# The lead-in of a recurrent-memory layer: fewer and larger DMA stores on one queue, and fewer warming products in the layer before it

## The chip, the cores and the metric

The kernel runs on one core of one Trainium2 chip. The metric is the device time of one execution in microseconds (us). The core has five engines that each run their own list of instructions: TensorE (PE) with its weight loads (PEld), VectorE (DVE), ScalarE (ACT), GpSimd (POOL) and SyncE (SP). DMAs are issued by an engine as one of its instructions (here almost all by SP, and some by ACT) and are carried by 16 shared DMA engines. An instruction that waits for a semaphore holds up all that stands behind it on its engine, a DMA issue among them.

## The reference

Four residual layers in a row, A, B, A, B, on x of 2048 rows by 640 columns, each behind a layer norm without weights:

```python
x = x + _A_ref(_layernorm(x), A_wq, A_wk, A_wv, A_wo, A_beta)
x = x + _B_ref(_layernorm(x), B_mem0, B_Wq, B_Wk, B_Wv, B_Wo, B_seg_len)
x = x + _A_ref(_layernorm(x), ...)
x = x + _B_ref(_layernorm(x), ...)
```

A is attention with a compressive memory: 32 heads of 20, four segments of 512 rows; in each, causal-masked softmax attention, and beside it a read of a memory matrix that the earlier segments' keys and values were added to; the two are mixed by a gate, sigmoid of beta. B is a recurrent-memory transformer, 32 heads of 128, in 64 segments of 32 rows:

```python
mem = mem0                                    # 8 tokens
for s in range(64):
    h = concatenate([mem, x[32*s : 32*s+32]])  # 40 tokens
    q, k, v = h @ Wq, h @ Wk, h @ Wv
    p = softmax(where(mask, q @ k.T * scale, -1e9))
    o = (p @ v) @ Wo
    mem = o[:8]                               # feeds the next segment
    outs.append(o[8:])
```

The 64 steps of B depend on one another through `mem`, so they run one after the other.

## The kernel before

**A.** The work runs over 32 groups of four heads (`NGR`), in a loop over `g` from 0 to `NGR + 1`; each group's scores (S, tiles `a_S`) are made in one turn, and its transposed scores, exponentials and products with V (T, tiles `a_T`, `a_PT`, `a_PV`) two turns later. So in the last two turns, `g >= NGR`, only T rounds are left: the drain. `unread(k)` sends k products of 128x256 to PE into a tile `a_W` that nothing reads. It is called at the start of the layer, ahead of each of the four blocks of transposes of the normed input (`seg_tr`), in the drain ahead of each round (nine times in a layer), and in a few other places. The order of ACT, DVE and POOL in A comes from due times (`KeyOrder`, `A_LAGS`): an instruction's key is its turn plus a lag by kind.

**B.** One step: projections of K and Q in two halves each (`b_Ka`, `b_Qa`, `b_Kb`, `b_Qb`), transposes of them (`b_TPak` and so on), scores `b_SP`, V in two halves (`b_Va`, `b_Vb`), the transposed probabilities (`b_PTP`), the product with V (`b_OTP`), the output product with Wo (`b_OPS`), and the new memory's transposes (`b_MT`) into `b_HX`, from which the next step's projections read. In B the order of PE, ACT, DVE and POOL is the order in which the instructions are written (`_OrdNC`); SP's is the scheduler's.

A step carries 40 tokens but the step's products are made for 32 of them, the 8 of memory and the first 24. The last eight of each segment, the tails, don't depend on memory; their Q, K and V are made ahead of time, for eight segments at once, a batch T for segments 8T to 8T+7. `tail_unit` and `tail_evac` make a batch's Q and K in eight pieces, k = 0 to 7 (tile `b_tail` in PSUM, `b_tu` in SBUF), and store each into DRAM at `QKd`. `vtail_unit` and `vtail_evac` do the same for V (`b_vtail`, then `b_vt` or `b_vts`), stored to `VTd`. Each step reads its own tails back: `tails_load` (tile `b_tl`), `tails_copy` (POOL, into `b_QZ` and `b_KT`), and `vtails_in` (four DMAs into rows of `b_Vth`).

**The lead-in of B.** Ahead of step 0 a stretch of code is run once in each B layer: it loads and norms the first four groups of 128 rows (`ln_load`, `ln_norm`; `ln_spread` transposes a normed group into `b_HX` and `b_TX`, tile `b_lntps`), makes the Q and K tails of batch 0 in eight pieces, makes K and Q of step 0's input rows (`b_Kp`, `b_Qp`), loads Wo in eight pieces of 640 KB (`load_B_wo`, `b_wo`), loads the first tails, makes the V tails of batch 0 in eight pieces and V of step 0's input (`b_V`), reads V tails back, and makes the first piece of batch 1. All of these evictions alternate between ACT and DVE. The stores of the pieces are issued by ACT for half of them and by SP for the others:

```python
tail_evac(0, k, "act" if k % 2 == 0 else "dve", ..., (nc.sync if k % 2 else nc.scalar).dma_start)
...
vtail_evac(0, k, vtail_unit(0, k), "dve" if k % 2 == 0 else "act", vt_homes[k], (nc.scalar if k % 2 else nc.sync).dma_start)
```

Each of the eight V pieces is a [128, 256] tile and goes out in two stores of 64 partitions, sixteen in all. `OTdef` are two tiles of [128, 32, 32] that later steps use for deferred output products; during the lead-in they are free.

Of the kernel before, what the change touches and what calls it, by code (L numbers as in the profile page):

```python
# [19 lines left out]
BF16 = mybir.dt.bfloat16  # L20
# [224 lines left out]
def layer_A(nc, tc, C, W, x_src, x_dst, src_is_bf16, nseg=4, out_bf16=False, xb_dst=None, load_w=None, side_loads=None):  # L245
    SC = 1.0 / math.sqrt(20.0)
    nc_raw = nc
    nc = _OrdNC(tc, nc_raw, engines=("tensor",))
# [4 lines left out]
    with ExitStack() as ctx:  # L253
# [15 lines left out]
        wk = pool("a_wk", 2)  # L269
# [34 lines left out]
        def unread(k):  # L304
            W_ = pg.tile([128, 256], F32, name="a_W", tag="pg")
            for _ in range(k):
                nc.tensor.matmul(W_[:], lhsT=C.identb[:], rhs=C.negu[:].rearrange("p a k -> p (a k)"), start=True, stop=True, skip_group_check=True)
# [297 lines left out]
        for tt in range(4):  # L605
            K.base = 0.1 * tt - 100.0
            seg_norm(0, tt)
            K.base = None
            unread((14 if src_is_bf16 else 6, 4, 4, 4)[tt])
            seg_tr(0, tt)  # L610
        K.base = -90.0
        lw.send(K) if src_is_bf16 else None
# [83 lines left out]
        for g in range(NGR + 2):  # L696
            n, G = divmod(g, 8)
            for half in range(2):
                p, tp = 2 * g + half, 2 * g + half - 3
                for ph in range(2):  # L700
                    K.base = 4 * g + 2 * half + ph
                    todo = []
                    for what in VISITS[ph]:
                        kind, r = what[0], int(what[1])
                        if kind == "X":
                            X = s_mask(p, r) if g < NGR else t_tile()
                            if g < NGR:
                                todo.append(("S", p, r, X, 0))
                            if 0 <= tp - 1 < 2 * NGR:
                                todo.append(("T", tp - 1, r, X, 256))  # L710
                        elif kind == "S" and g < NGR:
                            todo.append((kind, p, r, s_mask(p, r), 0))
                        elif kind == "T" and 0 <= tp < 2 * NGR:
                            todo.append((kind, tp, r, t_tile(), 0))
                    for step in range(2):
                        for kind, p_, r, X, o0 in todo:
                            if step == 0 and g >= NGR:
                                unread(4)
                            f = (s_mm, s_max)[step] if kind == "S" else (t_round, t_exp)[step]
                            f(p_, r, X, *((o0,) if o0 else ()))  # L720
                    if g < NGR and half == 1 and ph == 1:
                        negmax_rows(g)
                    if g == NGR + 1 and half == 1 and ph == 0:
                        last_turns(0, 4)
                        for tt in range(4):
                            last_oT(tt, 0, 4, K("last").vector if tt < 2 else nc.scalar)
                    filler(g, 2 * half + ph)
                    if side_loads is not None and g < NGR:
                        if g + half + ph == 0:
                            build_gates(nc, st, W, side_loads[1])  # L730
                        side_loads[0](4 * g + 2 * half + ph, GS[g]["kT"])
# [45 lines left out]
def layer_B(nc, tc, C, W, x_src, xb_src, x_dst, mem0, B_Wv, B_Wo, nsteps=64, out_bf16=False, tag=""):  # L777
    SCB = 1.0 / math.sqrt(128.0)
    nc_raw = nc
    nc = _OrdNC(tc, nc_raw, engines=ORDER_ENGINES)  # L780
# [3 lines left out]
    VTd = tc.dram_tile([nsteps, 8, 4096], BF16, name=f"b_VTd{tag}")  # L784
    with ExitStack() as ctx:
# [8 lines left out]
        kqp = pool("b_kqp", 4)  # L794
        W.wo = pool("b_wo", 1).tile([128, 32, D], BF16, name="b_wo")
        st = pool("b_state", 1)
        w2 = pool("b_w2", 2)
        wk = pool("b_wk", 1)
# [30 lines left out]
        HX, TX, QT, KT, VH = {}, {}, {}, {}, {}  # L829
# [83 lines left out]
                nc.sync.dma_start(VH[s - 1][32 * j:32 * j + 8, :, :],  # L913
                                  VTd[s].rearrange("t (b n e) -> t n b e", b=2, e=512)[:, j, :, :])

        tail_ps, vts = {}, {}

        def tail_unit(T, k, i0, i1, shared=False):
            proj, hg = divmod(k, 4)
# [13 lines left out]
        def tail_evac(T, k, eng, home=None, dma=nc.sync.dma_start):  # L933
            proj, hg = divmod(k, 4)
            pool_, tg = home or (wk, "tu")
            tu = pool_.tile([128, 8, 8, 8], BF16, name="b_tu", tag=tg)
            evac(eng, tu[:].rearrange("p s h t -> p h s t"), tail_ps[0][:].rearrange("p h (s t) -> p h s t", t=8),
                 None if proj else SCB)
            o = 256 * proj + 64 * hg
            dma(QKd[8 * T:8 * T + 8, :, o:o + 64].rearrange("s p f -> p s f"), tu[:].rearrange("p s h t -> p s (h t)"))  # L940

        def vtail_unit(T, k, c0=0, c1=NCH, ps=None):
            b4, ch = divmod(k, 2)
            if ps is None:
                ps = ps_tile([128, 256], F32, "b_vtail")
            for c in range(c0, c1):
                for q in range(4):
                    n = 2 * b4 + q // 2
                    nc.tensor.matmul(ps[32 * q:32 * q + 32, :], lhsT=TX[T][:, c, 4 * (q % 2):4 * (q % 2) + 4, :].rearrange("p s t -> p (s t)"),
                                     rhs=W.wv[:, c, 512 * n + 256 * ch:512 * n + 256 * ch + 256],  # L950
                                     start=(c == 0), stop=(c == NCH - 1), tile_position=(0, 32 * q), skip_group_check=True)
            return ps

        def vtail_evac(T, k, ps, eng, home=None, dma=nc.sync.dma_start):
            b4, ch = divmod(k, 2)
            if isinstance(home, int):
                if home == 0:
                    vts[0] = wk.tile([128, 5, 256], BF16, name="b_vts", tag="OTsb")
                vt = vts[0][:, home, :]
            else:  # L960
                pool_, tg = home or (wk, "vt")
                vt = pool_.tile([128, 256], BF16, name="b_vt", tag=tg)[:]
            evac(eng, vt, ps[:])
            for jj in range(2):
                o = 512 * (2 * b4 + jj) + 256 * ch
                dma(VTd[8 * T:8 * T + 8, :, o:o + 256].rearrange("s t f -> (s t) f"), vt[64 * jj:64 * jj + 64])
# [29 lines left out]
                nc.sync.dma_start(HX[0][:, c, 1, 0:8], mem0[:, 128 * c:128 * c + 128].rearrange("t p -> p t"))  # L996
        for k in range(8):
            tail_unit(0, k, 0, 8, shared=True)
            tail_evac(0, k, "act" if k % 2 == 0 else "dve", (((kqp, "kq"),) * 4 + ((w2, "QT"), (w2, "KT"), (wk, "tu"), (w2, "Vth")))[k],
                      (nc.sync if k % 2 else nc.scalar).dma_start)  # L1000
            if k in (0, 2) and n0 > 2:
                ln_norm(2 + k // 2)
            if k in (3, 5) and ln_ready:
                ln_spread(ln_ready.pop(0))
        cols = cols_of(0)
        jobs = [(nm, b) for b in range(2) for nm in ("K", "Q")]
# [13 lines left out]
        XO, XOd = init_state()  # L1020
        tails_copy(0, tails_load(0))
        Vth = VH[-1] = w2.tile([128, 2, 512], BF16, name="b_Vth", tag="Vth")
        vt_homes = [0, 1, 2, 3, 4] + [(wk, x) for x in ("PTa", "PTb", "E0")]
        for k in range(8):
            vtail_evac(0, k, vtail_unit(0, k), "dve" if k % 2 == 0 else "act", vt_homes[k],
                       (nc.scalar if k % 2 else nc.sync).dma_start)
        for b in range(2):
            ps = thin_mm(cols, W.wv, b, "b_V")
            evac("act" if b == 0 else "dve", Vth[:, b, :], ps[:])
# [372 lines left out]
```

## Time and profile before

| what | value |
|---|---|
| three runs | 2700.09, 2691.12, 2696.44 us |
| median | 2696.44 us |
| profiled execution, its own time | 2692.14 us |
| its span | 2690.4 us |
| mean granted TensorE clock | 0.997 |

By the trace, the first A layer fills about the first 342 us, the first B runs to about 1341, the second A to about 1683, and the second B to the end. A step of B is about 15 us. The stretches that the change touches are the first 20 us and the last 12 us of each A layer, and the lead-in of each B layer, which are the stretches 342 to 400 and 1683 to 1740. A window row of the profile gives the busy time of each engine, the clock that was granted to TensorE as a share of full speed, and how busy the DMA engines were; a chain row gives one piece of work and its duration, on the path that was followed back from the end of the window; a row with `[5.82 <-issue]` says how long the engine was idle ahead of it and what ended that.

### The profile page before, as it was taken

The numbers are of one execution on the slowest core, as the hardware profiler recorded it, in microseconds if no ns is written. First come the engines' busy times: TensorE is split into PE (matmuls) and PEld (weight loads), VectorE is DVE, ScalarE is ACT, GpSimd is POOL, SyncE is SP. The second block draws the span as 40 slices with busy tenths as digits, with TensorE's granted clock in tenths as the row PEclk, the third lists the DMA queues.
The fourth block names the chain that finished last, engine by engine and source line by source line (L and its number), as shares of the span: only waits on it lengthen the run. The fifth ranks groups of instructions, "written<-read, shape, count | busy, mean of one in ns | idle before, by whom it ended". The sixth has DMA issues, their size and how long they took to land.

```text
span 2690.4 us, 147288 instructions
## 1 busy us (share of the span) xinstructions
PE 2576.7 (96%) x65632; PEld 1699.2 (63%) x65632; DVE 1698.4 (63%) x4562; ACT 1583.1 (59%) x3718; POOL 710.0 (26%) x1631
## 2 busy tenths in 40 slices
PE   7999989999999999999989999899999999999998
PEld 5556566666666666666655566666666666666665
DVE  8999845555555555555589998455555555555554
ACT  6988835454555555554479898355555555555543
POOL 5777611111111111111156776111111111111110
PEclk9999999999999999999999999999999999999999
DMA  4122451222222222121120113511212121211110
GB/s 155 45 79 80 139 166 41 44 44 43 44 45 43 45 43 44 41 41 31 54 89 22 61 51 138 164 40 40 43 39 44 41 43 41 42 40 41 38 26 19
DMA packets 326620, 156.37 MB, mean 58 GB/s; under 512 B 246240, under 2 KB 310880, under 8 KB 324192
## 3 DMA queue, kind: packets, MB, share of 16 engines
q1 hardware_dynamic: 316384, 145.38, 21.3%
q8 instruction: 513, 8.40, 1.4%
q10 hardware_dynamic: 9600, 1.57, 0.4%
q14 instruction: 123, 1.01, 0.1%
HBM read 95.15 MB, written 51.71 MB: 55 GB/s over the span
## 4 chain that ended last, share of the span: by engine, by line
PE 79%; DVE 11%; ACT 5%; DMA 2%; issue 2%; SPq 1%; POOL 0%; ACTq 0%; DVEq 0%; POOLq 0%
PE b_OPS L109 11%; PE b_tail L109 5%; DVE a_nm L138 5%; PE b_Qa L109 5%; PE b_Ka L109 5%; PE b_Kb L109 5%; PE b_Qb L109 5%; PE b_Va L109 5%; PE b_Vb L109 5%; PE b_SP L109 4%; PE b_OTP L109 4%; PE b_OPSd L109 3%; PE b_PTP L109 3%; PE b_vtail L109 3%; ACT a_PT L138 3%; PE a_S L109 2%
## 5 line engine op out<-in xcount | busy, mean ns | idle before, releaser
L109 PEld LDWEIGHTS <-b_HX 128*32 128x32 bf16 x15360 | 427.9, 97 | 343.0 <-issue 12.4
L109 POOL TENSOR_TENSOR b_Pm<-b_E,b_rs 128x96 bf16<-128x96 bf16 x128 | 63.6, 497 | 1430.7 <-ACT b_Vth L109 1079.3
L138 DVE TENSOR_REDUCE a_nm<-a_S 128x2 f32<-128x512 f32 (+3 forms) x512 | 394.9, 815 | 27.6 <-PE a_S L109 20.1
L138 ACT ACTIVATE a_PT<-a_T 128x1024 bf16<-128x1024 f32 (+1 forms) x384 | 344.3, 901 | 32.0 <-PE a_T L109 24.2
L109 PE MATMUL b_OPS<-b_wo,b_OTsb 128*32 128x320 bf16 x8192 | 309.5, 301 | 10.4 <-issue 7.6
L109 PEld LDWEIGHTS <-b_OTsb 128*32 128x32 bf16 x8192 | 202.0, 97 | 95.7 <-DVE b_OTsb L109 24.3
L109 DVE CAST b_HX<-b_MT 128x8 bf16<-128x8 f32 x372 | 63.8, 172 | 274.2 <-PE b_MT L109 269.3
L138 POOL TENSOR_SCALAR_AFFINE_SELECT a_PT<-a_PT 128x256 bf16<-128x256 bf16 x380 | 188.7, 505 | 128.5 <-ACT a_PT L138 127.2
L109 ACT CAST b_msb<-b_OPS 128x64 bf16<-128x64 f32 x378 | 69.4, 256 | 237.7 <-PE b_OPS L109 237.6
L109 ACT CAST b_kq<-b_Kb 128x512 bf16<-128x512 f32 x128 | 75.0, 586 | 202.6 <-PE b_Kb L109 202.6
L109 DVE COPY b_KT<-b_TPak 128x128 bf16<-128x128 bf16 x128 | 28.8, 225 | 228.8 <-PE b_TPak L109 228.8
L109 DVE TENSOR_SCALAR b_kq<-b_Qa 128x512 bf16<-128x512 f32 x128 | 88.6, 692 | 130.3 <-PE b_Qa L109 127.2
L109 PE MATMUL b_Ka<-b_wk,b_HX 128*32 128x512 bf16 x2520 | 160.1, 381 | 6.2 <-ACT b_vt L109 6.2
L109 PE MATMUL b_Va<-b_wv,b_HX 128*32 128x512 bf16 x2520 | 161.0, 380 | 0.0
L109 PE MATMUL b_Qa<-b_wq,b_HX 128*32 128x512 bf16 x2520 | 159.9, 381 | 1.1 <-ACT b_Vth L109 1.1
L109 PEld LDWEIGHTS <-b_kq 128*128 128x128 bf16 x2080 | 116.9, 98 | 68.8 <-ACT b_kq L109 55.6
L109 PE MATMUL b_Vb<-b_wv,b_HX 128*32 128x512 bf16 x2520 | 160.3, 379 | 0.0
L109 PE MATMUL b_Kb<-b_wk,b_HX 128*32 128x512 bf16 x2520 | 159.5, 380 | 0.0
L109 PE MATMUL b_Qb<-b_wq,b_HX 128*32 128x512 bf16 x2520 | 158.8, 379 | 0.0
L109 DVE CAST b_OTsb<-b_OTP 128x160 bf16<-128x160 f32 (+1 forms) x384 | 122.5, 374 | 39.7 <-PE b_OTP L109 39.5
L109 ACT ACTIVATE b_E<-b_SP 128x320 bf16<-128x320 f32 (+1 forms) x256 | 81.1, 368 | 108.8 <-PE b_Va L109 100.0
L109 PE MATMUL b_vtail<-b_wv,b_TX 128*32 128x256 bf16 x2880 | 136.9, 271 | 3.9 <-issue 3.9
(211 smaller groups left out, 5786.1 us busy)
## 6 DMA issues: line engine op xcount, KB each, us to landing
b_tl<-b_QKd SPq DMA_DIRECT2D x128, 128.0 KB
b_QKd<-b_tu SPq DMA_DIRECT2D x120, 128.0 KB
b_wv<-in_B_Wv_dram SPq DMA_DIRECT2D x10, 1024.0 KB
b_wo<-in_B_Wo_dram SPq DMA_DIRECT2D x16, 640.0 KB
b_Vth<-b_VTd SPq DMA_DIRECT2D x512, 16.0 KB
b_XO<-xres SPq DMA_DIRECT2D x256, 30.0 KB
b_VTd<-b_vt SPq DMA_DIRECT2D x228, 32.0 KB
xres<-a_xnew SPq DMA_DIRECT2D x19, 320.0 KB
```

What stands on the lines that cost most here:

```text
L109: r = f(*a, **k)
L138: r = f(*a, **k)
```

## The change

It has three parts. First, `unread` at the start of A: in the first A layer (`src_is_bf16`) the fourteen products ahead of the first block of transposes go; in the second, six become four; the fours ahead of the other blocks stay. Second, in the drain of A, `unread(4)` ahead of each round becomes `unread(2)`. Third, the lead-in of B: all eight stores of Q and K tails are issued by SP; the eight pieces of V tails are gathered four by four in the two `OTdef` tiles, and each tile is stored with two DMAs of 64 partitions and 1024-byte runs (128 KB each), on SP, after the fourth and the eighth piece; and the two remaining `ln_spread` come after pieces 5 and 7 instead of 3 and 5.

```diff
-            unread((14 if src_is_bf16 else 6, 4, 4, 4)[tt])
+            if tt or not src_is_bf16:
+                unread(4)
             seg_tr(0, tt)
...
                             if step == 0 and g >= NGR:
-                                unread(4)
+                                unread(2)
...
-            if isinstance(home, int):
-                if home == 0:
-                    vts[0] = wk.tile([128, 5, 256], BF16, name="b_vts", tag="OTsb")
-                vt = vts[0][:, home, :]
-            else:
-                pool_, tg = home or (wk, "vt")
-                vt = pool_.tile([128, 256], BF16, name="b_vt", tag=tg)[:]
+            if home is not None:
+                vt = OTdef[k // 4][:].rearrange("p a c -> p (a c)").rearrange("p (k f) -> p k f", f=256)[:, k % 4]
+                evac(eng, vt, ps[:])
+                if k % 4 == 3:
+                    src = OTdef[k // 4][:].rearrange("p a c -> p (a c)").rearrange("p (b f) -> p b f", f=512)
+                    dst = VTd[0:8, :, 512 * (k - 3):512 * (k + 1)].rearrange("s t (b j f) -> j (s t) b f", b=2, j=2)
+                    for jj in range(2):
+                        nc.sync.dma_start(dst[jj], src[64 * jj:64 * jj + 64])
+                return
+            vt = wk.tile([128, 256], BF16, name="b_vt", tag="vt")[:]
             evac(eng, vt, ps[:])
...
             tail_unit(0, k, 0, 8, shared=True)
             tail_evac(0, k, "act" if k % 2 == 0 else "dve", (((kqp, "kq"),) * 4 + (...))[k],
-                      (nc.sync if k % 2 else nc.scalar).dma_start)
...
-            if k in (3, 5) and ln_ready:
+            if k in (5, 7) and ln_ready:
                 ln_spread(ln_ready.pop(0))
...
-        vt_homes = [0, 1, 2, 3, 4] + [(wk, x) for x in ("PTa", "PTb", "E0")]
         for k in range(8):
-            vtail_evac(0, k, vtail_unit(0, k), "dve" if k % 2 == 0 else "act", vt_homes[k],
-                       (nc.scalar if k % 2 else nc.sync).dma_start)
+            vtail_evac(0, k, vtail_unit(0, k), "dve" if k % 2 == 0 else "act", 0)
```

More of the change, by code (lines that the diff above doesn't have):

```diff
@@ L914, in vtails_in @@
                                   VTd[s].rearrange("t (b n e) -> t n b e", b=2, e=512)[:, j, :, :])
-        tail_ps, vts = {}, {}
+        tail_ps = {}
         def tail_unit(T, k, i0, i1, shared=False):
@@ L998, in layer_B @@
             tail_unit(0, k, 0, 8, shared=True)
-            tail_evac(0, k, "act" if k % 2 == 0 else "dve", (((kqp, "kq"),) * 4 + ((w2, "QT"), (w2, "KT"), (wk, "tu"), (w2, "Vth")))[k],
-                      (nc.sync if k % 2 else nc.scalar).dma_start)
+            tail_evac(0, k, "act" if k % 2 == 0 else "dve", (((kqp, "kq"),) * 4 + ((w2, "QT"), (w2, "KT"), (wk, "tu"), (w2, "Vth")))[k])
             if k in (0, 2) and n0 > 2:
                 ln_norm(2 + k // 2)
-            if k in (3, 5) and ln_ready:
+            if k in (5, 7) and ln_ready:
                 ln_spread(ln_ready.pop(0))
```

## The prediction

> **What bounds the kernel now.** I read the page first: its shares of engines, its chain, its costliest groups. Then I read the stages that the change touches, each by its own views: the chain, the waits and short windows.
>
> ```profile
> PE 2576.7 (96%) x65632; PEld 1699.2 (63%) x65632; DVE 1698.4 (63%) x4562; ACT 1583.1 (59%) x3718; POOL 710.0 (26%) x1631
> PE 79%; DVE 11%; ACT 5%; DMA 2%; issue 2%; SPq 1%; POOL 0%; ACTq 0%; DVEq 0%; POOLq 0%
> L109 PE MATMUL b_Ka<-b_wk,b_HX 128*32 128x512 bf16 x2520 | 160.1, 381 | 6.2 <-ACT b_vt L109 6.2
> ```
>
> TensorE (PE) is busy for 96% of the span and carries 79% of the chain, so only stages where PE idles, or does work nobody reads, can give much. The third row shows such a place: all of b_Ka's idle time, 6.2 us, was ended by ScalarE (ACT) writing b_vt, a V tail. That happens only in the lead-in of B, once in each B layer. The chain of waits through the first lead-in:
>
> ```profile
> 371.99 8.02 DMA b_wo<-in_B_Wo_dram
> ...
> 381.65 2.32 PE b_Ka L109 x20
> 383.98 2.13 PE b_Qa L109 x20
> 386.11 1.72 PE b_Kb L109 x20
> 387.83 1.08 PE b_Qb L109 x20
> ...
> 390.04 0.82 PE b_SP L109 x65
> ...
> 395.11 0.45 PE b_OTP L109 x29
> ...
> 395.96 2.56 PE b_OPS L109 x64
> ```
>
> The last load of b_wo releases ACT, not PE. ACT then issues two DMAs, evicts one V tail, and only then can PE start step 0 of B. The same place by windows, and in the timelines of PE, ACT, SP and POOL:
>
> ```profile
> 374.00:378.00 4.00, 3.44 (x88) 2.72 (x81) 1.12 (x2) 0.37 (x1) 0.00 (x0) 1.00 1.06 377
> 378.00:382.00 4.00, 0.35 (x4) 0.13 (x7) 0.00 (x0) 0.37 (x1) 0.00 (x0) 0.81 0.80 274
> 382.00:386.00 4.00, 4.00 (x44) 1.81 (x40) 0.00 (x0) 1.67 (x3) 0.87 (x3) 0.50 0.22 56
> 381.65 2.32 PE L109 MATMUL b_Ka<-b_wk,b_HX 128*32 128x512 bf16 x20 [4.21 <-ACT b_vt L109]
> 381.23 0.37 ACT L109 CAST b_vt<-b_vtail 128x256 bf16<-128x256 f32 x1 [5.82 <-issue]
> 366.70 7.10 SPq L768 DMA_DIRECT2D b_wo<-in_B_Wo_dram x5
> 388.19 2.85 SPq L913 DMA_DIRECT2D b_Vth<-b_VTd x4
> 382.20 0.53 POOL L109 COPY b_QZ<-b_tl 128x128 bf16<-128x128 bf16 x2 [23.39 <-DMA b_tl<-b_QKd]
> ```
>
> The columns of a window are length, busy time of PE, PEld, DVE, ACT and POOL, granted clock, DMA share, GB/s. From 378 to 382 PE does 0.35 us of work; then its granted clock is 0.50, and b_Ka takes 2.32 us where b_Qb, of the same size and at the end of the row, takes 1.08. ACT was idle for 5.82 us with "issue" as the reason: it sat on its own DMA issues.
>
> **The lead-in of B1.** The change takes four stores of Q/K tails and eight of V tails off ACT's queue, so the eviction at 381.23 no longer stands behind an issue that waits for b_wo. Three things go. First the wait itself, 4.21 us ahead of b_Ka. Second the slow clock: b_Ka to b_Qb take 2.32 + 2.13 + 1.72 + 1.08 = 7.25 us, four at 1.08 are 4.32, so 2.9 us. Third some of PE's earlier idling on unevicted V tails: in the window 374 to 378 it is 4.00 − 3.44 = 0.56 us; I take 0.5. Together 7.6.
>
> What is late next is the data of step 0. All eight Q/K stores now go ahead of b_wo's loads 1 to 7 on SP, and b_tl is queued behind those loads. In the old order b_tl was there at 382.20 and POOL's copies of it end at 383.07 (0.87 busy in the window). The scores would now want it at 390.04 − 7.6 = 382.4. The bytes are the same and the DMA share stands at 1.06 while they move, so I expect the same landing, give or take 2 us: a new wait of 0.7 (0 to 2.7). b_Vth is now issued ahead of the stores of the next tails, but only when its four V stores and POOL have finished; PV wants it at 395.11 − 7.6 = 387.5, and in the old order it was issued at 388.19. The four issues take 2.85 us, and the stores they depend on are four of 128 KB instead of sixteen of 32 KB. I take 0.3 (0 to 1.5). The merged stores are the one operation that the trace lacks: the same bytes, so between nothing and, if each goes like a b_wo load, 8.02 us of delay to the first b_Vth; nearest are the existing 32 KB ones, hence the small value. Moving the two spreads of normed rows behind later tails keeps PE, DVE and ACT instructions; it costs nothing at step 0, since these rows (the third and fourth group of four segments) belong to steps 8 to 15. VectorE gains no instruction, only another target tile. Gain 7.6 − 0.7 − 0.3 = 6.6 (7.6 − 2.7 − 1.5 = 3.4 to 7.6).
>
> **The lead-in of B2.** Here no slow clock was seen; the waits of PE are:
>
> ```profile
> PE b_Ka L109 <- ACT b_vt L109: 2.0, 1, 2.0
> PE b_Qa L109 <- ACT b_Vth L109: 1.1, 1, 1.1
> PE b_V L109 <- issue: 0.7, 1, 0.7
> PE b_OPS L109 <- ACT b_OTsb L109: 0.6, 1, 0.6
> ACT b_vt L109 <- issue: 6.5, 1, 6.5
> ```
>
> All four come from an ACT held for 6.5 us by issues, or (the last) by a b_tu whose store stood behind b_Vth on SP and now stands ahead of it: 2.0 + 1.1 + 0.7 + 0.6 = 4.4. The spread that moves back may let a tail start earlier; I count nothing for it, against a new wait like that of B1, and take 4.4. For the upper end I add idle time like that of B1's window twice, 1.1; for the lower I take off half of B1's worst new waits, (2.7 + 1.5) / 2 = 2.1 (2.3 to 5.5).
>
> On the DMAs that moved from ACT to SP, the Trainium skill, "DMA: Bandwidth & Descriptors", section "Issuing engines are not separate DMA queues", says that starting DMAs from several engines saves only the time to initiate them, usually small. By that rule giving up ACT's queue costs nearly nothing, and by the row of 5.82 us ACT as an issuer costs far more than it saves; this agrees, and the sum stands without it.
>
> **The drain of A.** In the last groups PE runs without a gap, and the unread products lie on the chain:
>
> ```profile
> 329.45 0.60 PE a_W L109 x4
> ...
> 338.30 0.54 PE a_W L109 x4
> L138 ACT ACTIVATE a_PT<-a_T 128x1024 bf16<-128x1024 f32 (+1 forms) x9 | 7.3, 882 | 3.3 <-PE a_T L109 3.3
> ```
>
> Nine rounds lose two products each. A round of four is 0.54 to 0.60, so two are at most 0.27 to 0.30, and 0.21 (an estimate: b_Ka gives 1.08 us for twenty products of 512 columns that run four side by side, so 0.216 for 512 columns in one row, the same as two of 256) at least: 9 × 0.21 = 1.9. The exponentials' idle time of 3.3 us, ended by a_T, shrinks with it, and they can become the limit in the last rounds: three of 0.88 are 2.65 us, near what PE will need for three rounds. I take 1.6 (0.3 to 2.4) for each A layer; both drains look alike on the chain, so 3.2. What follows, A's last turns and B's first stage, moves up whole: it hangs on A's outputs, not on a load.
>
> **The start of A.** In A1 the fourteen products go, but the start hangs elsewhere. The first row is PE's group of unread products from 8 to 12 us, the others are of the chain:
>
> ```profile
> L109 PE MATMUL a_W<-c_negu,c_identb 128*128 128x256 bf16 x15 | 3.4, 404 | 8.6 <-DVE c_negu L72 8.6
> 16.60 0.23 ACT a_beta_e L213
> 16.83 0.48 ACT a_qT L138
> 17.32 0.04 issue
> 17.36 0.87 PE a_KV L109 x10
> ...
> 19.63 0.50 PE a_S L109 x4
> 20.13 0.97 PE a_QP L109 x4
> ```
>
> The order of instructions after the change has a_qT ahead of a_beta_e on ACT, which waits for the load of beta and ran at 16.60, a_qT right behind it. PE then gets a_qT once its projection is there, about 1 us earlier. I take 0.9 (0 to 1.1). In A2 two products fewer lie in idle time, but a_kT goes ahead of a_qT on ACT; a copy is 0.48, so −0.2 (−0.45 to 0).
>
> **Sum.** 6.6 + 4.4 + 3.2 + 0.9 − 0.2 = 14.9 us. The profiled execution took 2692.14 us, its span being 2690.4, and lies 4.3 below the runs' median of 2696.44 and inside their 2691.12 to 2700.09. From the profiled time the sum gives 2677.2, from the median 2681.5; I take 2680, nearer to the median since that is what the result will be. No change would then be 2694.9. The lower ends of the terms add up to 3.4 + 2.3 + 0.6 + 0 − 0.45 = 5.9, the upper ones to 7.6 + 5.5 + 4.8 + 1.1 − 0 = 19.0. A measurement of this kernel can tell about 0.3%, 8.1 us.
>
> **Rivals.** (1) *The lead-in is bound by DMA.* b_wo's last load, b_tl and b_Vth land 3 to 5 us later since the stores now stand in one row ahead of the loads. For it: the DMA share of 1.06 at 374 to 378. Against: bytes are unchanged. At 4 us, B1 keeps 6.6 − 4 = 2.6 and B2, if half of it is felt there, 2.4: with 3.9 elsewhere 8.9, or 2686. Chance 0.16.
>
> (2) *A colder start of A1.* The fourteen products go ahead of all transposes. If PE's clock halves without them, a_KV, a_S and a_QP double, 0.87 + 0.50 + 0.97 = 2.3 us lost, and the sum is 12.6, or 2682.3. For it: 0.50 was granted after the idle stretch at 378, and fifteen products took 3.4 us at the start, 0.23 each, against 0.54 / 4 = 0.135 in the drain, so PE's first 3.4 us are slow and somebody has to spend them. Against: without the products the transposes can begin earlier and spend them, and these three come behind all transposes. Chance 0.18. The Trainium skill, "TensorE: Matmul & The Clock Gate", section "What's actually happening", says that the array falls to half clock after an idle window of about 3.4 us and returns after as much busy time; by that rule, which the 4.2 us idle and the 0.50 agree with, halving the drain's products costs nothing (no gap there is near it), while the start of A could run cold.
>
> (3) *Slower: SP holds back b_wo.* Loads 1 to 7 each stand behind an SP wait for a store to land. In the old order five of them left within 7.10 us. If they leave one per 6 us instead, the last lands at 366.7 + 7 × 6 = 408.7, 12.7 us after b_OPS's 395.96 began; in both layers 25.4, less 3.9 elsewhere, on 2694.9: 2716.4. It decides from a last landing at 388.4 (395.96 − 7.6), and the whole turns slower by 0.3% if it lands some 6 us after 395.96 in both, at 402 (12 − 3.9 = 8.1). Against: the stores in front are short and land while the projections run. Chance 0.08.
>
> (4) *Nothing changes in the lead-in*, since the evictions wait for the OTdef tiles or another engine takes over as the holder. Then 3.9 remains: 2691. Chance 0.07.
>
> **How the numbers follow.** Forecast 0.51, and the rivals 0.18, 0.16, 0.08 and 0.07. Faster by over 0.3% (below 2696.44 − 8.1 = 2688.3) are the forecast, the colder start and half of rival 1: 0.77. Within 0.3% are its other half and rival 4: 0.15. Slower 0.08. The range goes from the upper ends' 2694.9 − 19.0 = 2675.9 to the lower ends' 2689.0, with some 3 to 5 on each side for the spread of the runs: 2671 to 2692. Rivals 1 and 2 lie inside, rival 4 at its edge and rival 3 outside.
>
> **What would show it.** In the profile after: b_Ka of step 0 without the 6.2 us behind ACT b_vt; the clock above 0.9 in the 12 us after it; b_Ka to b_Qb at 1.08 each; POOL's b_QZ within 3 us of b_Qb's end; the drain's a_W rows as x2 of some 0.3 us; a_qT before a_beta_e. I am wrong if PE waits at b_SP for POOL b_KT or at b_OTP for b_Vth by over 3 us, or at b_OPS for b_wo at all.

## The result and the profile after

The changed kernel takes 2689.93 us (median of 20 runs, 2682.54 to 2699.71) where the kernel before takes 2696.65 (20 runs beside it). The ratio is 0.9975, with a 95% interval of 0.9967 to 0.9982. So it is faster, by 6.7 us, where 14.9 were forecast: less than half. All later ratios are against runs of the kernel before on the same chip in the same group; chips differ by up to 11 us, so times of different groups aren't compared.

The profiled execution took 2689.07 us, its span is 2687.3. From its page, the rows that answer to those shown of before:

```profile
PE 2567.8 (96%) x65516; PEld 1700.9 (63%) x65580; DVE 1695.2 (63%) x4562; ACT 1582.9 (59%) x3718; POOL 707.4 (26%) x1631
PE 79%; DVE 11%; ACT 6%; issue 2%; DMA 1%; POOL 0%; SPq 0%; ACTq 0%; DVEq 0%; POOLq 0%
L109 PE MATMUL b_Ka<-b_wk,b_HX 128*32 128x512 bf16 x2520 | 159.2, 379 | 0.0
```

The 6.2 us that b_Ka waited for ACT are gone, as forecast. The chain through the first lead-in, and windows of it with the timelines of SP and POOL, show what stands there now:

```profile
373.74 2.23 issue
375.97 1.25 PE b_V L109 x17
377.23 2.10 PE b_tail L109 x40
379.33 1.19 PE b_vtail L109 x16
380.51 1.28 PE b_Ka L109 x17
381.79 1.08 PE b_Qa L109 x18
...
386.16 0.60 PE b_SP L109 x49
...
391.84 0.41 PE b_OTP L109 x26
...
396.21 1.08 PE b_Ka L109 x20
```

```profile
372.00:376.00 4.00, 1.77 (x47) 0.83 (x39) 0.38 (x1) 0.96 (x2) 0.00 (x0) 1.00 1.06 373
376.00:380.00 4.00, 4.00 (x73) 2.99 (x77) 0.69 (x1) 0.59 (x1) 0.00 (x0) 0.67 1.09 366
```

```profile
357.02 9.92 SPq L941 DMA_DIRECT2D b_QKd<-b_tu x8
367.00 9.15 SPq L769 DMA_DIRECT2D b_wo<-in_B_Wo_dram x7
376.25 1.65 SPq L903 DMA_DIRECT2D b_tl<-b_QKd x1
387.11 3.02 SPq L914 DMA_DIRECT2D b_Vth<-b_VTd x4
385.22 0.52 POOL L109 COPY b_QZ<-b_tl 128x128 bf16<-128x128 bf16 x2 [27.79 <-DMA b_tl<-b_QKd]
```

b_Ka of step 0 now starts at about 380.4 instead of 381.65. Ahead of it PE sat for 2.23 us in b_V with nothing to wait for but its own issue; then its clock was 0.67. b_Ka takes 1.28 on the chain, b_Qa 1.08 again. On SP the eight Q/K stores take 9.92 us in a row, each waiting for its eviction, and b_wo's seven loads start only at 367.00; before, load 1 was issued at 361.14. So b_tl's copies start at 385.22, where they started at 382.20 (46.1 us after the end of A instead of 41.1), and end just as the scores want them. In the second lead-in they are too late:

```profile
PE b_SP L109 <- POOL b_KT L109: 1.5, 1, 1.5
PE b_vtail L109 <- issue: 0.8, 1, 0.8
PE b_OTP L109 <- DMA b_Vth<-b_VTd: 0.6, 1, 0.6
```

The drain of A and the start of A1, from their chains:

```profile
328.98 0.38 PE a_W L109 x2
...
333.25 0.32 PE a_W L109 x2
...
335.54 1.95 ACT a_PT L138 x2
...
338.13 1.00 PE a_PV L109 x40
```

```profile
9.60 7.75 DMA a_beta_bf<-in_A_beta_dram
17.35 0.02 issue
17.38 0.23 ACT a_beta_e L213
17.60 0.18 ACT a_Kn L138
...
19.26 0.50 PE a_S L109 x4
```

From the end of the last a_YP to the end of the last a_PV the drain takes 11.71 us before (329.42 to 341.13) and 10.18 after (328.95 to 339.13), in the second A layer 11.72 and 10.19. That is 1.53 each, nearly the forecast 1.6, with ACT's exponentials on the chain at the end. In the start a_qT is out of the chain, but a_Kn now stands behind a_beta_e, whose load landed at 17.35; in this pair of profiles a_S starts 0.37 us earlier and the drain 0.47. Over all profiles of this study, the drain begins at 328.80 us in the median of the thirteen with the new start and at 329.75 in the median of the six with the old one: 0.95 earlier, close to the forecast 0.9.

One yardstick serves for all kernels below: from the end of A's last a_PV to the start of b_Ka of step 1, read from PE's timeline in each lead-in. It covers the whole lead-in with step 0, and leaves out the 64 steps, whose lengths scatter by up to 1.9 us each over the profiles of this study. Each value is of one execution, and two profiles of the same code differ in it by up to 2.8 us.

| kernel | first lead-in, us | second | ratio to before (95% interval) |
|---|---|---|---|
| before | 58.2 | 57.3 | 1 |
| changed | 56.9 | 56.6 | 0.9975 (0.9967 to 0.9982) |
| changed, again | 55.9 | 56.3 | 0.9975 (0.9965 to 0.9984) |
| before, drain 4 to 2 | 57.3 | 58.6 | 1.0000 (0.9991 to 1.0010) |
| before, drain 4 to 0 | 57.9 | 58.8 | 0.9992 (0.9983 to 1.0000) |
| before, start of A only | 57.1 | 58.7 | 1.0007 (0.9996 to 1.0018) |
| lead-in only | 54.3 | 54.6 | 0.9975 (0.9962 to 0.9988) |
| changed, spreads at 3 and 5 | 56.1 | 54.5 | 0.9965 (0.9953 to 0.9977) |
| changed, second a_xnb home | 55.2 | 54.9 | 0.9970 (0.9959 to 0.9981) |
| changed, b_wo held back | 62.1 | 62.5 | 1.0021 (1.0012 to 1.0030) |
| changed, b_wo written later | 54.4 | 55.3 | 0.9961 (0.9949 to 0.9973) |
| the same, spreads at 3 and 5 | 55.5 | 55.6 | 0.9973 (0.9963 to 0.9984) |
| the same, A's products put back | 53.7 | 53.8 | 0.9975 (0.9965 to 0.9986) |
| changed, half of Q/K stores on ACT | 53.1 | 52.9 | 0.9963 (0.9950 to 0.9975) |
| the same, again | 53.8 | 55.7 | 0.9953 (0.9937 to 0.9970) |
| the same, A's products put back | 51.5 | 54.1 | 0.9951 (0.9935 to 0.9968) |
| the same, and b_wo written later | 55.2 | 56.0 | 0.9967 (0.9957 to 0.9978) |
| changed, V stores not merged | 63.8 | 63.5 | 1.0025 (1.0014 to 1.0036) |
| changed, b_wo first | 64.3 | 65.0 | 1.0044 (1.0030 to 1.0057) |

### The profile page after: what moved, and what is told of

It reads as the page before. It is cut to its first block, busy times and chain, and to the rows that moved or that the text cites. A ratio compares the mean times of both kernels' runs of the same rounds, so it can differ in the third digit from the quotient of the medians.

```text
span 2687.3 us, 147084 instructions
## 1 busy us (share of the span) xinstructions
PE 2567.8 (96%) x65516; PEld 1700.9 (63%) x65580; DVE 1695.2 (63%) x4562; ACT 1582.9 (59%) x3718; POOL 707.4 (26%) x1631
## 3 DMA queue, kind: packets, MB, share of 16 engines
q14 instruction: 123, 1.01, 0.1%
## 4 chain that ended last, share of the span: by engine, by line
PE 79%; DVE 11%; ACT 6%; issue 2%; DMA 1%; POOL 0%; SPq 0%; ACTq 0%; DVEq 0%; POOLq 0%
PE b_OPS L109 11%; PE b_tail L109 6%; DVE a_nm L138 5%; PE b_Ka L109 5%; PE b_Qa L109 5%; PE b_Kb L109 5%; PE b_Qb L109 5%; PE b_Va L109 5%; PE b_Vb L109 4%; PE b_SP L109 4%; PE b_OTP L109 4%; PE b_vtail L109 3%; PE b_OPSd L109 3%; PE b_PTP L109 3%; ACT a_PT L138 3%; PE a_S L109 2%
## 5 line engine op out<-in xcount | busy, mean ns | idle before, releaser
L109 POOL TENSOR_TENSOR b_Pm<-b_E,b_rs 128x96 bf16<-128x96 bf16 x128 | 63.5, 496 | 1421.5 <-ACT b_Vth L109 1095.3
L109 DVE CAST b_HX<-b_MT 128x8 bf16<-128x8 f32 x372 | 63.5, 171 | 276.0 <-PE b_MT L109 270.6
L109 PEld LDWEIGHTS <-b_kq 128*128 128x128 bf16 x2080 | 116.8, 98 | 68.4 <-ACT b_kq L109 55.2
```

Of the source, the lines that this page charges most:

```text
L109: r = f(*a, **k)
```

## Experiments: which part brought the time

**The drain alone**, on the kernel before:

```diff
-                                unread(4)
+                                unread(2)
```

> The kernel before with only the drain of A changed (two unread products per round instead of four). My theory after the result: the drain itself gets about 1.5 us shorter in each A layer, but the gain is spent again ahead of B's first projections, since ACT's casts into the one a_xnb tile wait for the stores to xres_bf, and the eviction of the first Q tail stands behind them. So b_Kp of the first lead-in starts within 0.7 us of where it started (362.4), and the whole gains 0 to 2 us. The prediction's view as rival: the drains' gain arrives, 3.2 us in all, and b_Kp starts about 1.6 us earlier.

Measured: 1.0000 (0.9991 to 1.0010), at most 2.4 us gained; the prediction's 3.2 lies outside the interval. The drains take 10.18 us each, so the 1.5 us are gained there. Where they are lost this profile doesn't show. b_Kp starts at 362.85, where it started at 362.36, but the drain itself began 1.4 us later here (330.83 against 329.42). Counted from the drain's beginning, b_Kp comes 0.9 us earlier in the first lead-in and 3.7 in the second, and step 1 comes 2.4 and 0.3 earlier.

**The lead-in alone**: the changed kernel with `unread` at 14 / 6 and at 4 in the drain.

> The changed kernel with all its unread products put back as before, so only the lead-in of B is new. My theory: the wait of b_Ka for ACT is gone, but PE then waits 0.5 to 2.5 us for its own instructions at b_V and up to 1.5 us for b_tl's copies, and about 0.6 for b_Vth, in each lead-in, so that step 1 of B starts 1 to 2.5 us earlier than before relative to the end of A, and both lead-ins together gain 3 to 5 us. The prediction as rival: 11 us.

Measured: 0.9975 (0.9962 to 0.9988), the same ratio as the whole change. By the yardstick 3.9 and 2.7 us are gained, 6.6 together: more than my 3 to 5, less than the prediction's 11. Within the intervals, all of the measured gain is in this part.

**The start of A alone**, on the kernel before:

```diff
-            unread((14 if src_is_bf16 else 6, 4, 4, 4)[tt])
+            if tt or not src_is_bf16:
+                unread(4)
```

> The kernel before with only the unread products at the start of A changed (fourteen to none in the first A layer, six to four in the second). The prediction had 0.9 us gained in the first and 0.2 lost in the second; in the profiles of the changed kernel the first drain begins 0.5 us earlier (0.3 to 1). So 0 to 1 us faster than before, which this measurement can't tell from none; a slower start by the half clock would show as 1 us or more slower and a later beginning of the drain.

Measured: 1.0007 (0.9996 to 1.0018). Nothing that can be told from none, as expected. The interval still holds a gain of 1.1 us, so it doesn't refute the prediction's 0.9 − 0.2.

**No unread product in the drain**, on the kernel before:

```diff
                             if step == 0 and g >= NGR:
-                                unread(4)
```

> The kernel before without any unread product in the drain's rounds (none instead of four). If the drain's length reached the end, as the prediction had it, the whole would gain at least twice the prediction's 3.2 us, some 6 us or more (about 2689). My theory: the drain gets about 2 to 3 us shorter in each A layer (then ACT's exponentials are its limit) and the gain is absorbed at ACT's a_xnb casts as before, so the whole lies within 2 us of before, and from the end of the drain to step 1 of B takes 1 to 3 us longer than before's 58.2 and 57.3.

Measured: 0.9992 (0.9983 to 1.0000), 2.1 us. This isn't the test that I expected it to be: its drains take 10.18 us each, no shorter than with two products, so no more than the 3.1 us of the run with two could arrive, and those lie inside this interval. The yardstick's 58 to 59 us are no shorter than before's. The window 336 to 340 shows PE busy for 2.25 of 4 us and the clock at 0.85, then at 0.72; and on its chain there stand POOL's a_PT and a_Onat, then DVE's. So without any product PE runs empty and slow, and other engines set the drain's length.

```profile
336.00:340.00 4.00, 2.25 (x33) 1.76 (x30) 2.65 (x7) 3.06 (x5) 3.18 (x6) 0.85 0.80 255
340.00:344.00 4.00, 3.81 (x64) 3.16 (x63) 2.73 (x8) 1.48 (x5) 0.00 (x0) 0.72 0.30 125
```

## Experiments: what holds the lead-in now

**The spreads back behind tails 3 and 5**:

```diff
-            if k in (5, 7) and ln_ready:
+            if k in (3, 5) and ln_ready:
```

> The changed kernel with the two spreads of normed rows back behind tails 3 and 5. In the trace of the changed kernel PE idled 1.9 and 3.2 us ahead of the fifth Q/K tail and the granted clock fell to half for 3.4 us in both lead-ins. Theory: the moved spreads left PE without work there; with them back the clock stays at 1.0 in that stretch and b_Kp starts 0.7 to 1 us earlier in the first lead-in. Rival: the wait belongs to ACT's a_xnb casts alone, the spread only splits it, and b_Kp starts at the same time within 0.3.

Measured: 0.9965 (0.9953 to 0.9977), not separable from the changed kernel's 0.9975. PE still waits for ACT's b_tu (3.21 us in the first lead-in, 1.47 in the second), and the clock still fell once in each. My theory of the moved spreads was wrong.

**A second home for a_xnb**:

```diff
-            xnb = w1l.tile([128, D], BF16, name="a_xnb")
+            xnb = up.tile([128, D], BF16, name="a_xnb", tag="PT") if n_ == nseg - 1 and tt % 2 else w1l.tile([128, D], BF16, name="a_xnb")
```

> The changed kernel with a second home for every other a_xnb tile of A's last segment, so that ACT's cast needn't wait for the store before it. Theory: the idle 1.9 and 3.2 us of PE ahead of the fifth Q/K tail go (to under 0.8), the clock stays at 1.0 there, and b_Kp starts 2 us earlier in the first lead-in and 3 in the second; since b_wo's loads start earlier too, most of it reaches step 1 and the whole gains 3 to 5 us on the changed kernel (about 2685 to 2687 where the changed one has 2690). Rival: something else (the norm of the next rows) holds the tails and less than 1 us is gained.

Measured: 0.9970 (0.9959 to 0.9981). The wait for ACT is gone in both lead-ins, but in the first PE waits 2.61 us for DVE's b_tu instead, and b_SP waits 3.25 us for b_tl's copies in the second. Less gained than expected; the stage ahead of b_Kp has several chains of nearly the same length.

**The changed kernel again.**

> The changed kernel once more, for a second profile of the same code beside the three others of this group. The stretch from the end of A's drain to b_Kp, 23.1 and 24.1 us in its first profile but 21.4 to 21.7 and 20.5 to 20.7 in two kernels that have the same instructions there, should come out between 20.5 and 22.5 if the first profile's value was chance (the stores to xres_bf land in 2.6 to 3.8 us), and at 23 or more if it belongs to the code. Time some 0.25% below the kernel before.

Measured: 0.9975 once more. The stretch to b_Kp was 21.7 and 20.6 us, so the first profile's 23.1 and 24.1 were partly chance. But the waits for b_tl's copies are there again, 1.43 and 3.04 us (the second just over the 3 us by which the prediction would call itself wrong), and so are PE's waits named issue, 1.76 and 0.79.

**No b_wo load while the V tails run.** Load 0 stays; a small write after the last V tail makes the others wait:

```diff
+        nc.vector.memset(W.wo[0:1, 4:32, 0:1], 0.0)
+        for k in range(1, 8):
+            load_B_wo(nc, W, B_Wo, k)
```

> The changed kernel with b_wo's loads 1 to 7 held back until the last V tail is evicted, by a small write into their tile that they must wait for. While the V tails and b_V run, no b_wo load is under way. Theory: PE's waits named issue at b_V (2.2 us in the first lead-in of the changed kernel, 0.8 in the second) are its instructions, which come by DMA through the same busy engines; they go to below 0.3, and b_tl and b_Vth are there in time. Rival: they have another cause (PE's queue, the PSUM tile) and stay. Either way the last loads land later and b_OPS may wait for b_wo by up to 3 us, so the whole is 2 us faster to 4 us slower than the changed kernel.

Measured: 1.0021, slower by 5.6 us. But what it was made for came out clearly: no PE wait named issue over 0.4 us in the V tails and b_V of either lead-in, and b_Ka starts 36.4 and 35.8 us after the end of A, where the changed kernel needed 41.2 and 39.2, and 38.4 and 37.2 in its second profile. The loads themselves now stand ahead of b_Vth:

```profile
393.39 1.18 PE L109 MATMUL b_OTP<-b_PTa,b_Vth 32*128 32x40 bf16 x32 [7.82 <-DMA b_Vth<-b_VTd]
```

In the second lead-in a wait named issue (2.10 us) turns up later, in a stretch where the loads do run. The traces' DMA packets say what these waits are. The profile's instruction queue q8 moves 8.40 MB over the span in 513 packets of 16 KB, one for about 256 of PE's products and weight loads. In the nineteen profiles PE has 389 waits of over 0.4 us that are named issue, and each of them ends 1.0 to 1.7 us after such a packet has landed; in the changed kernel the packet lands at 374.65 and PE goes on at 375.97. So PE waits for its own instructions, and the rival (PSUM, PE's own queue) is out. That b_wo's loads make the packets late rests on this run, and how late varies: with half of the Q/K stores on ACT (below) the DMA share is 1.07 and 1.08 from 372 to 380 too, and the longest such wait there is 0.48 us. In the kernel before, waits of 1.04 and 1.28 us stand among the 64 steps too, in windows (832 to 836 and 909 to 913) whose DMA share is 0.21 and 0.15.

**b_wo's loads 1 to 7 written after the V tails**, so that b_tl stands behind load 1 on SP and the V stores ahead of loads 6 and 7:

> The changed kernel with b_wo's loads 1 to 7 written after the V tails; on SP b_tl then stands behind load 1 instead of load 7, and the V stores stand ahead of loads 6 and 7. Theory: the waits for b_tl's copies (1.5 us in the second lead-in) and for b_Vth (0.7 and 0.6) go, and the stretch from the end of the drain to step 1 gets 1 to 2.5 us shorter in the second lead-in and about 0.7 in the first; whole 2 to 3 us faster than the changed kernel. Rival: the DMA engines are full either way and b_OPS then waits for the last loads instead; nothing gained.

Measured: 0.9961 (0.9949 to 0.9973); 2.5 and 1.3 us shorter by the yardstick than the changed kernel's first profile, 1.5 and 1.0 than its second. No wait for b_tl's copies is left; one for b_Vth (0.91 us) is, and b_OPS to step 1 takes 5.2 us in the second lead-in where the changed kernel took 3.6. PE's waits there add up to 0.3 us; the granted clock is 0.50 from 1724 to 1726, behind the waits at b_OTP. No wait for b_wo shows, so the rival doesn't either.

**The same with the spreads at 3 and 5:**

> The changed kernel with both: b_wo's loads 1 to 7 written after the V tails, and the spreads back behind tails 3 and 5. Theory: the two gains add up, drain's end to step 1 in 54 and 53 us where the changed kernel took 56.9 and 56.6, the whole at about 2684 to 2686. Rival: they are the same gain, or swallowed by PE's waits for its instructions, and it stays at 2687 to 2690.

Measured: 0.9973 (0.9963 to 0.9984). The gains don't add up.

**Half of the Q/K stores back on ACT:**

```diff
-            tail_evac(0, k, "act" if k % 2 == 0 else "dve", (...)[k])
+            tail_evac(0, k, "act" if k % 2 == 0 else "dve", (...)[k],
+                      (nc.sync if k % 2 else nc.scalar).dma_start)
```

> The changed kernel with the four stores of the even Q/K tails back on ACT. Theory: the gain of the lead-in lies in the V tails' stores, since ACT's issues of Q/K stores stand ahead of little that PE waits for; b_Ka's wait stays away, and the time is within 1.5 us of the changed kernel. Rival: the Q/K stores on ACT hold b_kq's evictions, as they held ACT for 2.1 us at 360 in the kernel before, and half of the gain, 3 us, is lost.

> The changed kernel with the four stores of the even Q/K tails back on ACT, a second time, as the companion of the three others of this group. If the first result (0.37% below the kernel before, no wait for b_tl's copies in either lead-in, drain's end to step 1 in 53.1 and 52.9 us) belongs to the code, it comes again: 0.3 to 0.45% below, no wait for POOL b_KT over 0.5 us, 52 to 54 us.

Measured: 0.9963 (0.9950 to 0.9975), and in a second group 0.9953 (0.9937 to 0.9970). In the group that ran both, the median is 2675.99 us with half on ACT and 2680.66 with all on SP. I had thought these stores didn't matter; they do, and moving them to SP was a loss. By the yardstick 53.1 and 52.9 us (53.8 and 55.7 again), against 56.9 and 56.6 (55.9 and 56.3 again). Counted from the end of A, b_tl's copies start after 41.9 and 40.0 us (42.7 and 42.9 again); in the changed kernel after 46.1 and 45.5 (45.5 and 45.1 again), and before after 41.1 and 41.3. PE waits for b_tl's copies in no lead-in of the two profiles. SP's timeline and a window say why:

```profile
356.92 3.22 SPq L941 DMA_DIRECT2D b_QKd<-b_tu x2
360.19 2.17 SPq L769 DMA_DIRECT2D b_wo<-in_B_Wo_dram x1
...
365.82 6.36 SPq L769 DMA_DIRECT2D b_wo<-in_B_Wo_dram x5
372.29 1.46 SPq L903 DMA_DIRECT2D b_tl<-b_QKd x1
380.92 0.53 POOL L109 COPY b_QZ<-b_tl 128x128 bf16<-128x128 bf16 x2 [23.73 <-DMA b_tl<-b_QKd]
```

The window 360 to 364, in the kernel before, the changed one, and this one in turn (the columns as in the prediction; the DMA share is the last but one):

```profile
360.00:364.00 4.00, 4.00 (x114) 3.18 (x115) 1.24 (x2) 1.38 (x5) 0.00 (x0) 1.00 1.33 255
```

```profile
360.00:364.00 4.00, 4.00 (x102) 3.04 (x102) 0.69 (x1) 1.71 (x4) 0.00 (x0) 0.96 0.79 138
```

```profile
360.00:364.00 4.00, 3.67 (x75) 2.07 (x75) 0.69 (x1) 2.17 (x6) 0.00 (x0) 1.00 1.36 203
```

With all eight stores on SP the DMA engines have 0.79 of a full load there, since SP stands at stores whose tails aren't made yet while loads that wait for nothing stand behind. With four on ACT, SP gets to load 1 at 360.19, and b_tl's copies start 4.3 us earlier (380.92 against 385.22).

**That, and A's unread products put back:**

> The version with the even Q/K stores on ACT and all unread products of A put back as in the kernel before: the lead-in's part alone. Theory: of the drains' 1.53 us each, the first is mostly lost ahead of b_Kp (PE's wait for b_tu was 0.8 to 1.5 us with the long drain and 1.8 to 2.1 with the short one) and the second arrives, so it is 1 to 3 us slower than its companion with the short drains. Rival (the prediction): the drains and the start arrive whole, 3 to 4 us slower. Rival (all absorbed): the same within 1 us.

Measured: 0.9951 (0.9935 to 0.9968), beside 0.9953 for its companion: no difference shows, but each interval reaches over 4 us to either side, so this pair alone doesn't exclude the prediction's 3.9. PE's waits between the end of A and 362, in this kernel and then in its companion with the short drain:

```profile
PE b_tail L109 <- ACT b_tu L109: 0.5, 1, 0.5
```

```profile
PE b_tail L109 <- ACT b_tu L109: 2.0, 1, 2.0
```

In the first lead-in most of the 1.5 us gained in the drain comes back as a longer wait at the fifth Q/K tail: with the new lead-in it is 0.5 to 1.1 us in three profiles with the long drain and 1.8 to 2.1 in nine with the short one, on average 1.1 us more.

**Both healings at once:**

> Both of the two faster versions at once: even Q/K stores on ACT, and b_wo's loads 1 to 7 written after the V tails (b_tl then stands behind load 3 on SP instead of load 7). If the two heal different waits, 1 to 2 us more than either; if, as I think, both heal the same one, b_tl's lateness, it is at the same 0.35 to 0.4% below the kernel before.

Measured: 0.9967 (0.9957 to 0.9978), not faster than either alone, as expected of two healings of one wait.

**The later b_wo with A's products put back:**

> The faster version (b_wo's loads 1 to 7 written after the V tails) with all unread products of A put back as in the kernel before. If the shorter drains (1.53 us each by the profiles) and the start reach the end, it is 3 to 4 us slower than without them (the faster version was 0.39% below the kernel before, this one would be 0.25% below); if they are absorbed, it stays at 0.35 to 0.4% below.

Measured: 0.9975 (0.9965 to 0.9986). Taken with 0.9961 of another group this looks like 3.7 us for the drains and the start, but the intervals overlap. The yardstick, which leaves the drains out, is 0.7 and 1.5 us longer without the products (54.4 and 55.3 against 53.7 and 53.8), so most of what the drains gave is taken back before step 1. The same holds on average for the three forms of the new lead-in that were profiled with both drains (as changed, b_wo later, half on ACT): with the short drains the yardstick is 1.4 us longer in each lead-in, nearly the 1.5 gained.

**V stores not merged:** sixteen of 32 KB on SP from the same two tiles.

```diff
-                if k % 4 == 3:
-                    ...
+                for jj in range(2):
+                    o = 512 * (2 * b4 + jj) + 256 * ch
+                    nc.sync.dma_start(VTd[0:8, :, o:o + 256]..., vt[64 * jj:64 * jj + 64])
```

> The changed kernel with sixteen stores of V tails, 32 KB each, on SP, instead of four of 128 KB; staging in the same two tiles. SP took 6.8 us for six such stores in the kernel before. Theory: SP needs 8 to 14 us more for them, all behind b_tl and ahead of b_Vth, so that the product with V of step 0 waits 5 to 10 us for b_Vth in each lead-in and the whole is slower than the kernel before by 4 to 12 us. Rival: they are issued while b_wo's loads are under way and cost below 2 us.

Measured: 1.0025 (1.0014 to 1.0036), slower than before by 6.7 us, as the theory had it. SP needs 14.57 us for the sixteen where the four took 3.40, and b_Vth follows:

```profile
377.17 14.57 SPq L962 DMA_DIRECT2D b_VTd<-b_OTdef x16
391.90 3.09 SPq L914 DMA_DIRECT2D b_Vth<-b_VTd x4
```

**All b_wo loads ahead of the Q/K stores, all on SP:**

```diff
         load_B_wv(nc, W, B_Wv)
+        for k in range(8):
+            load_B_wo(nc, W, B_Wo, k)
```

> The changed kernel with all eight b_wo loads written ahead of the Q/K tails: on SP the eight loads now stand ahead of the eight Q/K stores, which all stay on SP. If what costs is that the stores hold back the loads, and with them b_tl, then b_wo is done some 5 us earlier, b_tl's copies are in time (no wait of PE for POOL b_KT), and the whole comes to 0.35 to 0.5% below the kernel before, like the versions with half of the Q/K stores on ACT. If what costs is the stores' own issue on SP, b_tl is as late as in the changed kernel, and it stays at 0.25%.

Measured: 1.0044 (1.0030 to 1.0057), slower. The question isn't answered this way, because another wait took over: the Q/K stores, now behind the loads, hold the tiles in which b_Kp is evicted.

```profile
377.49 0.61 PE L109 MATMUL b_TP<-c_identb,b_kq 128*128 128x128 bf16 x4 [11.26 <-ACT b_kq L109]
```

## Why the prediction was right and wrong

Right were the direction and the stall it was built on: b_Ka's 6.2 us behind ACT went, and the b_Ka to b_Qb of step 0 are back at about 1.08 (b_Ka 1.28, at a clock of 0.80 from 380 to 382). Right were also the size of the drain's cut (1.53 for 1.6), the first A layer's start as far as the drain's beginning (0.95 in the medians for 0.9), and the merged stores as harmless: they are what makes the move to SP possible at all. The second A layer's start isn't decided: this pair of profiles has 0.1 lost for the forecast 0.2, but from the last step of B to the drain's beginning all profiles scatter between 339.3 and 343.6 us.

Wrong were two steps; by the runs they cost up to 3.2 and 3 to 6 of the 8.2 us that are missing.

First, "What follows, A's last turns and B's first stage, moves up whole". It doesn't: the drain alone gave 0 (at most 2.4 us), and with the new lead-in the yardstick grows by about what the drains gave. So the forecast's 3.2 us for the drains come to nothing that could be measured; the start's 0.9 − 0.2 are too small for these intervals to find or to refute. In the first lead-in the place is shown for about 1.1 of 1.5 us: PE's wait for b_tu behind ACT's casts grows by that. In the second it isn't settled; there the stage to b_Kp wasn't longer in most profiles, but later stages took the time back. In the old lead-in, where the drain was tested alone, the place stays open.

Second, "The bytes are the same ..., so I expect the same landing". This put 0.7 us on the eight Q/K stores standing ahead of b_wo on SP. b_tl's copies came 3.0 and 2.0 us later in the first lead-in of the two profiles of the changed kernel (385.22 and 384.19 against 382.20), although A ended 2.0 and 2.4 us earlier there, with waits of PE for its copies of 0 and 1.4 in the first lead-in and of 1.5 and 3.0 in the second. With half of the stores on ACT the change gives 0.37 and 0.47%, with all on SP 0.25% (twice): 3 to 6 us. This is rival 1 (the lead-in bound by late data), which had priced it at 6.0, by the cause that rival 3 named (SP holds b_wo back), far below that rival's 25.4.

With these two out, the remaining step, the lead-in, has a sum that fits: without the Q/K stores' move and without A's parts it gains 0.49% (0.32 to 0.65%), which is 13 us (9 to 18) where the prediction had 11 for both lead-ins; by the yardstick 6.8 and 3.2 us where it had 6.6 and 4.4. But that the sum fits is in part luck, since some of its terms were misread. The 0.5 for PE's idling in the window 374 to 378 was counted twice: PE's last product there ends at 377.44, and the 0.56 us up to 378 are the first part of the 4.21. The 0.7 at b_V in the second lead-in was named issue, so it was PE waiting for its instructions and not ACT held; in the changed kernel 0.84 of that kind are still there. And 4.21 and the 2.9 of slow clock are what one execution showed. The kernel with only the start of A changed has the old lead-in too, and there PE's waits are:

```profile
375.90 2.13 PE L109 MATMUL b_V<-b_wv,b_HX 128*32 128x512 bf16 x36 [2.41 <-issue]
381.71 1.26 PE L109 MATMUL b_Ka<-b_wk,b_HX 128*32 128x512 bf16 x20 [1.75 <-ACT b_vt L109]
```

With only the drain changed (4 to 2 and 4 to 0) they are 2.03 and 2.32 for instructions and 0 and 0.26 behind ACT. From b_Ka of step 0 to that of step 1 these three profiles take 15.4 to 15.5 us where the profile of before took 17.7, so the clock wasn't slow there; yet by the yardstick they are only 0.3 to 1.1 us shorter.

So a third cost, PE's waits for its own instructions, had no term of its own, and ACT's hold covered it in part: the more PE waited for instructions in the old lead-in, the less was left to wait for ACT. In the profile of before 0.49 us of it showed in the first lead-in and 0.72 in the second; in the changed kernel it is 2.23 and 0.84, again 1.76 and 0.79. So of the 4.21 us behind ACT only about half was to be had in the changed kernel.

The rule that I cited from the Trainium skill, "DMA: Bandwidth & Descriptors", section "Issuing engines are not separate DMA queues", says that several issuing engines save only the time to initiate a DMA. Here the measurement differs: the 3 to 6 us that half of the stores on ACT bring aren't spent on initiating. The same transfers on one engine stand in one row, and one that waits for its data holds back the ones that wait for nothing.

Rival 2 (a colder start of A1) didn't show: a_S starts 0.37 us earlier. The fastest kernels of this study are those with half of the Q/K stores on ACT (0.9953, and 0.9951 with A's unread products as they were); both are below the changed kernel's 0.9975, the intervals touching in part.

## What to carry to other kernels

When an issue queue is relieved by moving DMAs to another engine's queue, list what they stand ahead of there: an issue that waits for its data holds back every load behind it, and the price is read from the DMA share of the stretch in which they should have run. A stall that goes shows the next one, so look for waits that the old stall covered (here the instruction fetch and the copies of b_tl), and don't count a stage's gain as the end's before the waits between the two have been searched. And merge small stores before moving them: sixteen issues on one queue cost 14.6 us where four cost 3.4.

## What the runs showed of the hardware that was not expected

PE waited for its own instructions, 0.5 to 2.4 us at a time, in stretches where b_wo's loads filled the DMA engines (shares of 1.01 to 1.09), above all in the V tails and b_V with their many short products; with the loads held back these waits were gone there. All 389 waits of this kind over 0.4 us end 1.0 to 1.7 us after a 16 KB packet of the instruction queue has landed.

The granted clock halved after gaps shorter than I had thought: in the changed kernel it was 0.61 from 356 to 360, behind 1.87 us of idling, and 0.67 from 376 to 380, behind 2.23 (0.50 from 358 to 360 and from 378 to 380); in its second profile gaps of 1.98 and 1.76 us in the same places left it at 1.00, and a gap of 2.41 did so in the kernel with only the start of A changed. The Trainium skill, "TensorE: Matmul & The Clock Gate", section "What's actually happening", gives an idle window of some 3.4 us that runs freely; the trace agrees with a window whose start is chance, but the gaps that sufficed here are shorter. So near 2 us it is a matter of chance from one execution to the next, and perhaps part of the scatter in time.
